# A planned attention and Fourier-gate kernel on one core: first head pair split, loads moved to the GpSimd queue, bit rows padded, new DMA model and new warm filling in the planner

## The chip, the cores and the metric

The kernel runs on 1 core of one Trainium2 chip. The metric is device time in microseconds, lower is better. A run is "fast" or "slow" by its state; only fast runs are compared. The profile is one execution: PE is TensorE, PEld its weight loads, DVE is VectorE, ACT is ScalarE, POOL is GpSimd, SP is SyncE. "SPq" or "POOLq" is an engine's sequencer, which issues DMAs.

## The reference, cut to what matters

```
# 4 batches x 8 heads, 768 positions, head size 64
q_bits = (q @ proj) > 0 ; k_bits = (k @ proj) > 0          # 6 bits each
mask   = bucket(q_bits) == bucket(k_bits)
attn   = softmax(where(mask, q @ k.T / 8, -1e9)) ; x = attn @ v
p      = x @ w_proj                                        # x1, x2, x3
y      = x1 * irfft(rfft(x2) * rfft(filter)) * x3
out    = y @ w_out
```

The kernel works on 16 pairs of heads. Four pairs make a batch; when a batch's four pairs are normalised, its projection, Fourier and output matmuls fill TensorE beside the attention of the next pairs.

## The kernel before

The kernel is recorded first and then ordered: a planner (`plan`) simulates the engines with a cost per instruction and a latency per DMA, decides the order on every engine, and the program is issued in that order. Each engine works through its instructions in the order in which they were issued (a profile below shows VectorE standing 7.24 us before its next one), so a latency that the planner believes too short puts an instruction where its engine must stand and wait. These are the parts that matter.

```
# the DMA model of the planner
LATE = (2600.0, 1900.0)
    if ty == "InstDmaTransposeAnt":
        return 1700.0, LATE[0], False, 0.0
    if ty == "InstDMACopy":
        move = n * partitions * bytes / 200.0          # one pipe of 200 GB/s
        own, late = {"Pool": (560.0, ...), "Activation": (150.0, ...)}.get(eng, (520.0, LATE[1]))
        return own, late, False, move
...
            x = end + 650
            if form["move"]:
                dma = max(x, dma) + form["move"]       # all queues share it
                got = dma + form["late"] - 650

# all loads on the SP queue ("p")
LOADS, SMALL, LOADQ = "p", "p", "p"

# high and low fp16 parts of q and k, then one DMA transpose each into the rows pr_q, pr_k
    def turn_dma(g):
        for which in ("k", "q"):
            nc.sync.dma_start_transpose(row[which]..., HLS[g][which]...)

# bits of the buckets, written under the 64 rows of q and k by 4 DMAs of 12 partitions
        for i in range(4):
            nc.load(row[...][HD : HD + NBIT, i % 2, :], bt[32 * i : 32 * i + NBIT, :], SMALL)

# normaliser: row sums S -> lt -> reciprocal rl -> DRAM rdr -> broadcast R, then the product on VectorE
    def finish(g):
        ...
            nc.load(lt[:, par, :], S[r0 : r0 + 1, 0:SEQ], SMALL)
        nc.vector.reciprocal(rl, rl)
        nc.load(rdr.rearrange("h (p c) -> p h c", p=P), rl, SMALL)
        for par in range(2):
            nc.load(R[HD * par : HD * par + HD, :], rdr[par : par + 1, :].to_broadcast([HD, SEQ]), SMALL)
        nc.vector.scalar_tensor_tensor(U, in0=T[:, 0:SEQ], scalar=vsd, op0=ALU.add, in1=R, op1=ALU.mult)
...                                                    # cut
```

The softmax here doesn't subtract the row's maximum and nothing guards it: scores larger than these inputs give would overflow.

## Time and profile before

| | before |
|---|---|
| time, median of the first 3 runs | 463.43 us (461.94 to 465.23) |
| span of the profiled run, mean granted clock | 461.0 us, 0.978 |
| PE busy | 431.6 us (94%) |
| useful matmul time (columns at full rate, worked out) | 381 us |

Lines of the page of the kernel before: busy time of two engines, and the DMA queues (packets, MB, share of the 16 DMA engines' span). q1 is the SP queue, q10 the ScalarE queue, q0 the GpSimd queue.

```profile
PE 431.6 (94%) x2590; PEld 233.4 (51%) x2590; DVE 305.9 (66%) x552; ACT 252.8 (55%) x348; POOL 112.2 (24%) x117
...
q1 hardware_dynamic: 99472, 51.00, 43.3%
q10 hardware_dynamic: 1552, 0.39, 0.4%
...
q0 software_dynamic: 128, 0.04, 0.0%
```

Nearly all bytes go through one queue, SP's, in small packets: 51.00 MB in 99472 packets is 513 B each.

Stretches of the kernel before: the length, busy time (instructions) of PE, PEld, DVE, ACT and POOL, the granted clock, the DMA share and GB/s.

```profile
20.00:30.00 10.00, 8.66 (x47) 3.81 (x46) 5.25 (x9) 6.71 (x9) 0.61 (x1) 0.63 0.86 181
80.00:90.00 10.00, 9.18 (x37) 3.75 (x37) 9.04 (x18) 3.65 (x6) 2.71 (x5) 0.83 0.64 159
260.00:280.00 20.00, 20.00 (x140) 12.10 (x139) 15.93 (x39) 11.94 (x18) 4.26 (x4) 1.00 0.21 60
```

The late part keeps PE busy without a gap at full clock; the early part does not, and its busy time holds warm-up matmuls and slow-clock matmuls.

The chain of work that ended last, from 10 to 140 us, its DMA transposes alone: start, length from issue to landing in us, and which.

```profile
12.38 3.31 DMA pr_k<-hl
18.05 4.62 DMA pr_q<-hl
28.36 3.21 DMA pr_q<-hl
54.82 4.45 DMA pr_q<-hl
71.54 4.34 DMA pr_q<-hl
118.44 3.37 DMA pr_k<-hl
```

A transpose on the chain takes 3.2 to 4.6 us, 3.88 us in the mean of the six. How long VectorE stood before its product with R, in total, times and the longest:

```profile
DVE R L232 <- DMA R<-rdr: 14.6, 6, 6.6
```

And the issues of the bit rows on SP, duration in ns as least, median and most:

```profile
L232 SPq DMA_DIRECT2D pr_q<-bt x30: 717/780/918, 24.9 to 333.2; - x30
L232 SPq DMA_DIRECT2D pr_k<-bt x30: 714/720/1072, 26.8 to 334.8; - x30
```

### The profile page before, as it was taken

To read this page: it belongs to the slowest core of one execution; us is meant where nothing else is said; L and a number is where in the kernel's file an instruction comes from. 1 tells how busy PE (TensorE), PEld (TensorE's weight loads), DVE (VectorE), ACT (ScalarE), POOL (GpSimd) and SP (SyncE) were. 2 spreads that over 40 slices of the span, in tenths; PEclk is the share of its full clock that TensorE was granted. 3 is DMA by queue.
4 is the path that set the end of the run, shared out by engine and by line. 5 is a ranking of instruction groups with operands and counts; after the bars stand their busy time and mean duration, and the time that the engine had idled before them with its cause. 6 is when DMAs were issued, how large, how long until landed. Compare 5 with 4: busy or idle time off the path is not lost.

```text
span 461.0 us, 7071 instructions
## 1 busy us (share of the span) xinstructions
PE 431.6 (94%) x2590; PEld 233.4 (51%) x2590; DVE 305.9 (66%) x552; ACT 252.8 (55%) x348; POOL 112.2 (24%) x117
## 2 busy tenths in 40 slices
PE   7688987969899999999999999999999999999996
PEld 5244544425355456544455665544556664445652
DVE  4667687949593899734588879225677873279870
ACT  5679979358146752777565766665666632200102
POOL 4103297223031521212232211113242010122000
PEclk9789999879999999999999999999999999999999
DMA  9988679798845324765372323451010103100003
GB/s 273 201 213 207 159 213 251 165 202 216 201 110 148 86 58 76 183 162 155 79 135 71 75 71 74 141 131 48 3 40 2 34 4 107 66 0 1 0 2 137
DMA packets 101187, 51.88 MB, mean 113 GB/s; under 512 B 83520, under 2 KB 92816, under 8 KB 101152
## 3 DMA queue, kind: packets, MB, share of 16 engines
q1 hardware_dynamic: 99472, 51.00, 43.3%
q10 hardware_dynamic: 1552, 0.39, 0.4%
q8 instruction: 20, 0.33, 0.3%
q14 instruction: 15, 0.12, 0.1%
q0 software_dynamic: 128, 0.04, 0.0%
HBM read 32.02 MB, written 6.39 MB: 83 GB/s over the span
## 4 chain that ended last, share of the span: by engine, by line
PE 71%; DMA 12%; DVE 9%; ACT 3%; issue 3%; SPq 1%; DVEq 0%; ACTq 0%; POOLq 0%
PE x L232 24%; PE pv L232 10%; PE stp L232 9%; PE wout L232 9%; PE x2b L232 6%; PE x2a L232 6%; DMA pr_q<-hl 4%; PE zps L232 2%; DMA lt<-S 2%; ACT pt L232 2%; DMA w<-in_moe_w_proj_dram 2%; PE fdft L232 2%; DMA pr_k<-hl 1%; DMA R<-rdr 1%; DMA rdr<-rl 1%
## 5 line engine op out<-in xcount | busy, mean ns | idle before, releaser
L232 ACT ACTIVATE pt<-stp,nmatch 128x768 f16<-128x768 f32 x192 | 168.6, 899 | 65.1 <-PE stp L232 62.4
L232 PE MATMUL stp<-pr_q,pr_k 76*128 76x512 f16 (+1 forms) x384 | 96.3, 334 | 11.2 <-ACT pt L232 8.5
L232 PE MATMUL x<-xh,wph 128*128 128x384 f16 x256 | 83.4, 326 | 0.5 <-DVE bt L232 0.2
L232 PE MATMUL x<-xl,wph 128*128 128x384 f16 x256 | 83.4, 326 | 0.0
L232 PE MATMUL x<-xh,wpl 128*128 128x384 f16 x256 | 83.4, 326 | 0.0
L232 PE MATMUL pv<-pt,vt 128*128 128x257 f16 (+1 forms) x384 | 76.4, 333 | 1.4 <-DVE bt L232 1.4
L232 PEld LDWEIGHTS <-wph 128*128 128x128 f16 x512 | 49.7, 97 | 34.6 <-issue 2.2
L232 DVE SCALAR_TENSOR_TENSOR T<-S,cst_sb,pv 64x512 f32<-64x512 f32 x64 | 38.3, 608 | 36.8 <-ACT S L232 35.9
L232 PEld LDWEIGHTS <-pr_k 76*128 76x128 f16 x384 | 36.9, 99 | 49.8 <-issue 22.8
L232 POOL TENSOR_TENSOR xl<-R,xh 128x768 f16<-128x768 f32 x16 | 26.3, 1641 | 133.1 <-DVE xh L232 112.4
L232 PEld LDWEIGHTS <-vt 128*128 128x128 f16 x384 | 37.8, 99 | 29.8 <-issue 5.9
L232 ACT COPY S<-pv 64x512 f32<-64x512 f32 (+1 forms) x48 | 22.8, 476 | 43.1 <-PE pv L232 39.1
L232 PEld LDWEIGHTS <-wpl 128*128 128x128 f16 x256 | 25.0, 97 | 16.1
L232 POOL TENSOR_TENSOR vt<-nat_v,vt 128x768 f16<-128x768 f32 x16 | 26.2, 1641 | 17.9 <-ACT vt L232 17.0
L232 PEld LDWEIGHTS <-xh 128*128 128x128 f16 x192 | 18.7, 97 | 20.7 <-issue 0.3
L232 DVE TENSOR_SCALAR bt<-zps,cst_sb 128x384 f16<-128x384 f32 x30 | 17.5, 610 | 16.2 <-PE zps L232 15.7
L232 ACT ACTIVATE osb<-wout 128x512 f32<-128x512 f32 x24 | 14.3, 596 | 24.7 <-PE wout L232 24.6
L232 POOL CAST vt<-nat_v 128x768 f16<-128x768 f32 x11 | 9.0, 823 | 74.1 <-PE pv L232 74.1
L232 DVE SCALAR_TENSOR_TENSOR R<-T,vsd,R 128x768 f32<-128x768 f32 x16 | 16.2, 1012 | 14.6 <-DMA R<-rdr 14.6
L232 DVE SCALAR_TENSOR_TENSOR hl<-nat_k,hl 128x768 f16<-128x768 f32 x16 | 16.3, 1016 | 12.2 <-ACT hl L232 12.1
L232 DVE TENSOR_TENSOR fu<-x2b,x2s 128x512 f32<-128x512 f32 x12 | 8.3, 688 | 23.6 <-PE x2b L232 23.6
L232 ACT ACTIVATE hl<-nat_k 128x768 f16<-128x768 f32 x16 | 13.5, 844 | 14.7 <-DMA pr_k<-hl 9.1
(339 smaller groups left out, 673.5 us busy)
## 6 DMA issues: line engine op xcount, KB each, us to landing
nat_k<-in_k_dram SPq DMA_DIRECT2D x16, 384.0 KB
nat_v<-in_v_dram SPq DMA_DIRECT2D x16, 384.0 KB
R<-rdr SPq DMA_DIRECT2D x32, 192.0 KB
out_dram<-osb SPq DMA_DIRECT2D x24, 256.0 KB
nat_q<-in_q_dram SPq DMA_DIRECT2D x15, 384.0 KB
w<-in_moe_w_proj_dram SPq DMA_DIRECT2D x12, 256.0 KB
w<-in_moe_filter_fft_dram SPq DMA_DIRECT2D x6, 256.0 KB
w<-in_moe_w_out_dram SPq DMA_DIRECT2D x4, 256.0 KB
```

The costliest lines, as they stand in the source:

```text
L232: o["done"] = getattr(getattr(nc, o["lane"]), o["method"])(*[sub(x) for x in o["args"]], **{n: sub(x) for n, x in o["kw"].items()})
```

## The change

Its intent: start the first pair head by head so that scores begin earlier; take the big loads off the SP queue, where they stand between transposes and normaliser; issue bit rows faster; give the planner a DMA model closer to the machine; and keep TensorE's clock up with filler matmuls in smaller pieces, without an end time.

```
+ROWS = 16
-LATE = (2600.0, 1900.0)
+DMA_LATE = (900.0, 1400.0)
+DMA_SHARE = 1.4
...
-        return 1700.0, LATE[0], False, 0.0
+        return 1500.0, DMA_LATE[0], False, 1900.0
-        move = n * partitions * bytes / 200.0
+        size = min(_run(wr[0]), _run(rd[0]))
+        move = n * partitions * bytes / size
+        move *= max(9.0, 11.0 + 0.0362 * size) / 16.0
...
+        return own, DMA_LATE[1] + (600.0 if eng == "Pool" else 0.0), False, max(60.0, move)
...
-                dma = max(x, dma) + form["move"]
-                got = dma + form["late"] - 650
+            x = max(s + 500.0 if form["late"] == DMA_LATE[0] else end + 300.0, dma.get(e, 0.0))
+            move = form["move"] * (DMA_SHARE if any(dma[y] > x for y in dma if y != e) else 1.0)
+            dma[e] = x + move                          # one pipe per queue
+            got = max(end, dma[e]) + form["late"]
...
-LOADS, SMALL, LOADQ = "p", "p", "p"
-WARM_COLS, WARM_UNTIL, WARM_FILL = 256, 115000.0, 0.7
+BITQ, WQ = "p", "g"
+LOADS, SMALL, LOADQ = "g", "p", "g"
+WARM_COLS, WARM_GAP, WARM_FILL = (256, 128, 64), 350.0, (0.97, 0.7)
...
-        load_qk(0, "p", "s")
+        for par in range(2):
+            first_loads(par)                           # k on SP, q and the identity on ScalarE, half a pair each
         NATS[0]["v"] = nat_load(v, 0, "v", "p")
-        hilo(0)
         load_qk(1, None, None)
-        turn_pe(0)
-        zbits(0, True)
+        for par in range(2):
+            first_turn(par)                            # high/low, transpose, bits, thresholds of one head
...
-                row[...][HD : HD + NBIT, i % 2, :], bt[32 * i : 32 * i + NBIT, :], SMALL
+                row[...][HD : HD + ROWS, i % 2, :], bt[32 * i : 32 * i + ROWS, :], BITQ
...                                                    # cut
```

More of the change, by code (lines that the diff above doesn't have):

```diff
@@ L168, in scale, with lower @@
         ])
+    def lower(self, out, a, c, b, lanes="v"):
+        self.either(*[
+            lambda e={"v": self.vector, "g": self.gpsimd}[x]: e.scalar_tensor_tensor(
+                out, in0=a, scalar=c, op0=ALU.mult, in1=b, op1=ALU.subtract
+            )
+            for x in lanes
+        ])
     def load(self, out, in_, lanes=None):
@@ L185, in inline_tensor, with fill @@
         return self.core.inline_tensor(data, name=name)
+    def fill(self, nc, bank, n, sub):
+        w, z = self.warm
+        nc.tensor.matmul(bank[:, SEQ : SEQ + n], sub(w), sub(z[:, 0:n]))
     def issue(self, tc, order, place):
@@ L228, in issue @@
                 if k < 0:
-                    nc.tensor.matmul(self.warm[0](real[bank]), sub(self.warm[1]), sub(self.warm[2]))
+                    self.fill(nc, real[bank], -k, sub)
                     continue
@@ L272, in _cols, with _run @@
     return n
+def _run(ap):
+    n = 1
+    for step, k in reversed(list(ap.ap)[1:]):
+        if step != n:
+            break
+        n *= k
+    return n * (2 if "16" in str(ap.dtype) else 4)
 def _cost(ins, eng, rd, wr):
@@ L287, in _cost @@
     if ty == "InstDmaTransposeAnt":
-        return 1700.0, LATE[0], False, 0.0
+        return 1500.0, DMA_LATE[0], False, 1900.0
     if ty == "InstDMACopy":
-        move = n * list(wr[0].ap)[0][1] * (2 if "16" in str(wr[0].dtype) else 4) / 200.0
-        own, late = {"Pool": (560.0, LATE[1] + 200.0), "Activation": (150.0, LATE[1] + 500.0)}.get(
-            eng, (520.0, LATE[1])
-        )
-        return own, late, False, move
+        size = min(_run(wr[0]), _run(rd[0]))
+        move = n * list(wr[0].ap)[0][1] * (2 if "16" in str(wr[0].dtype) else 4) / size
+        move *= max(9.0, 11.0 + 0.0362 * size) / 16.0
+        own = {"Pool": 560.0, "Activation": 480.0}.get(eng, 480.0)
+        if eng == "SP" and size == 2 * SEQ:
+            own = 600.0
+        return own, DMA_LATE[1] + (600.0 if eng == "Pool" else 0.0), False, max(60.0, move)
     big = [a for a in rd if _cols(a) > 1]
@@ L316, with HI_LANES, LO_LANES @@
 NQK = 4
-LOADS, SMALL, LOADQ = "p", "p", "p"
-WARM_COLS, WARM_UNTIL, WARM_FILL = 256, 115000.0, 0.7
+BITQ, WQ = "p", "g"
+LOADS, SMALL, LOADQ = "g", "p", "g"
+WARM_COLS, WARM_GAP, WARM_FILL = (256, 128, 64), 350.0, (0.97, 0.7)
 T_SET = (1.5, 3.0, 5.0)
+def HI_LANES(g, which):
+    return "v" if g == 0 and which == "q" else "s"
+HL1_AT = -1.52
+def LO_LANES(g, which):
+    return "v"
 def PROJ_AT(b, x):
@@ L390, in plan @@
             last[x] = g[0]
+            for m in g[1:]:
+                deps[m].add(g[0])
         if ops[g[0]]["method"] == "matmul" and len(g) > 2 and not ops[g[0] + 1]["with_"]:
@@ L422, in _order @@
     port = {"DVE": 0.0, "Pool": 0.0}
-    dma = 0.0
+    dma = {}
     forced = {}
@@ L525, in _order @@
             gap = s - free[e]
-            if book.warm is not None and s < WARM_UNTIL and gap > 350.0 and before:
+            if book.warm is not None and gap > 40.0 and before:
                 w0 = free[e]
-                room = w0 + WARM_FILL * gap
-                while True:
-                    c = WARM_COLS / 2.4
-                    if active.get(int(w0 // 3413) - 1, 0.0) < 1640.0:
-                        c *= 2
-                    if w0 + c > room:
-                        break
-                    active[int(w0 // 3413)] = active.get(int(w0 // 3413), 0.0) + WARM_COLS / 2.4
-                    extra.append((w0, -1, before))
-                    w0 += c
+                while w0 < s:
+                    cold = active.get(int(w0 // 3413) - 1, 0.0) < 1640.0
+                    if not cold and gap < WARM_GAP:
+                        break
+                    room = free[e] + WARM_FILL[0 if cold else 1] * gap - w0
+                    c = [n for n in WARM_COLS if n / (1.2 if cold else 2.4) <= room]
+                    if not c:
+                        break
+                    x = int(w0 // 3413)
+                    active[x] = active.get(x, 0.0) + c[0] / 2.4
+                    extra.append((w0, -c[0], before))
+                    w0 += c[0] / (1.2 if cold else 2.4)
             mode[0] = o["mode"]
@@ L552, in _order @@
         if form["late"]:
-            x = end + 650
-            if form["move"]:
-                dma = max(x, dma) + form["move"]
-                got = dma + form["late"] - 650
-            else:
-                got = end + form["late"]
+            x = max(s + 500.0 if form["late"] == DMA_LATE[0] else end + 300.0, dma.get(e, 0.0))
+            move = form["move"] * (DMA_SHARE if any(dma[y] > x for y in dma if y != e) else 1.0)
+            dma[e] = x + move
+            got = max(end, dma[e]) + form["late"]
         for t in o["touch"]:
@@ L646 @@
     ident = cp.tile([P, P], FP16, name="ident")
-    nc.gpsimd.dma_start(ident, id_d.ap())
     for r0 in (0, HD):
@@ L658 @@
     wps = psS.tile([P, 1024], FP32, tag="s", name="stp")
-    nc.warm = (lambda t: t[:, SEQ : SEQ + WARM_COLS], warm[:, 0:P], warm[:, 0:WARM_COLS])
+    nc.warm = (warm[:, 0:P], warm)
     nc.at = -2.9
-    nc.tensor.matmul(nc.warm[0](wps), nc.warm[1], nc.warm[2])
+    nc.tensor.matmul(wps[:, SEQ:1024], *nc.warm)
     NPR = 3
@@ L709, in hilo @@
         HLS[g] = {}
-        nc.at = g - 1.6
+        nc.at = g - 1.6 if g > 1 else HL1_AT
         for which in ("k", "q"):
@@ L713, in hilo @@
             hl = hlp.tile([P, 2 * NCH, 2, HD], FP16, tag=f"hl_{which}", name="hl")
-            if g == 0 and which == "q":
-                nc.vector.tensor_scalar(hl[:, :, 0], nat, QKS, None, ALU.mult)
-            else:
-                nc.scalar.mul(hl[:, :, 0], nat, QKS)
-            nc.vector.scalar_tensor_tensor(
-                hl[:, :, 1], in0=nat, scalar=QKS, op0=ALU.mult, in1=hl[:, :, 0], op1=ALU.subtract
-            )
+            nc.scale(hl[:, :, 0], nat, QKS, HI_LANES(g, which))
+            nc.lower(hl[:, :, 1], nat, QKS, hl[:, :, 0], LO_LANES(g, which))
             HLS[g][which] = hl
@@ L730, in turn_dma @@
             )
-    def turn_pe(g):
-        row = prs[g % NPR]
-        for which in ("k", "q"):
-            for par in range(2):
-                tp = psW.tile([P, SEQ], FP16, tag="w", name="tp")
-                for n in range(NCH):
-                    nc.tensor.transpose(
-                        tp[:, ts(n, P)],
-                        HLS[g][which][:, NCH * par + n].rearrange("p s d -> p (s d)"), ident,
-                    )
-                if par:
-                    nc.vector.tensor_copy(row[which][:, par], tp)
-                else:
-                    nc.scalar.copy(row[which][:, par], tp)
@@ L747, in zbits, with first_loads @@
-    def zbits(g, direct=False):
+    def first_loads(par):
+        hs = slice(NCH * par, NCH * par + NCH)
+        for which, src in (("k", k), ("q", q)):
+            if par == 0:
+                NATS[0][which] = natp.tile(
+                    [P, 2 * NCH, HD], FP32, tag="qk", name=f"nat_{which}", bufs=NQK
+                )
+            t_ = NATS[0][which]
+            if which == "k":
+                nc.load(
+                    t_[:, hs].rearrange("p n d -> p (n d)"),
+                    src[0, par].rearrange("(p n) d -> p (n d)", n=NCH), "p",
+                )
+            else:
+                nc.load(t_[:, hs], src[0, par].rearrange("(n p) d -> p n d", p=P), "s")
+            if par == 0 and which == "q":
+                nc.load(ident, id_d.ap(), "s")
@@ new lines, in first_turn @@
+    def first_turn(par):
+        row = prs[0]
+        hs = slice(NCH * par, NCH * par + NCH)
+        for which in ("k", "q"):
+            nc.at = -2.0 + 0.5 * par
+            nat = NATS[0][which]
+            if par == 0:
+                HLS[0][which] = hlp.tile([P, 2 * NCH, 2, HD], FP16, tag=f"hl_{which}", name="hl")
+            hl = HLS[0][which]
+            nc.scale(hl[:, hs, 0], nat[:, hs], QKS, "sv")
+            nc.vector.scalar_tensor_tensor(
+                hl[:, hs, 1], in0=nat[:, hs], scalar=QKS, op0=ALU.mult, in1=hl[:, hs, 0],
+                op1=ALU.subtract,
+            )
+            tp = psW.tile([P, SEQ], FP16, tag="w", name="tp")
+            for n in range(NCH):
+                nc.tensor.transpose(
+                    tp[:, ts(n, P)], hl[:, NCH * par + n].rearrange("p s d -> p (s d)"), ident
+                )
+            for hf in range(2):
+                cs = slice(HALF * hf, HALF * hf + HALF)
+                nc.copy(row[which][:, par, cs], tp[:, cs], "sv")
+        zps = psW.tile([P, HALF], FP32, tag="w", name="zps")
+        srcs = [(w_, hf) for w_ in ("k", "q") for hf in range(2)]
+        for s_ in range(2):
+            for i, (which, hf) in enumerate(srcs):
+                nc.tensor.matmul(
+                    zps[32 * i : 32 * i + 32, :], pjh[:, s_],
+                    row[which][:, par, HALF * hf : HALF * hf + HALF],
+                    start=(s_ == 0), stop=(s_ == 1),
+                )
+                nc.ops[-1]["with_"] = bool(s_ or i)
+        for i in (0, 2, 3, 1):
+            which, hf = srcs[i]
+            r_ = slice(32 * i, 32 * i + ROWS)
+            nc.vector.tensor_scalar(
+                row[which][HD : HD + ROWS, par, HALF * hf : HALF * hf + HALF],
+                zps[r_, :], thresh[r_, :], BIT, ALU.is_gt, ALU.mult,
+            )
@@ L748, in zbits @@
+    def zbits(g):
         row = prs[g % NPR]
@@ L763, in zbits @@
                     nc.ops[-1]["with_"] = bool(hf or s_ or i)
-        if not direct:
-            for hf in range(2):
-                nc.vector.tensor_scalar(
-                    bt[:, HALF * hf : HALF * hf + HALF], zs[hf], thresh, BIT, ALU.is_gt, ALU.mult
-                )
-        if direct:
-            for i in (2, 0, 3, 1):
-                for hf in range(2):
-                    r_ = slice(32 * i, 32 * i + NBIT)
-                    nc.vector.tensor_scalar(
-                        row[("q", "k")[i // 2]][HD : HD + NBIT, i % 2, HALF * hf : HALF * hf + HALF],
-                        zs[hf][r_, :], thresh[r_, :], BIT, ALU.is_gt, ALU.mult,
-                    )
-            return
+        for hf in range(2):
+            nc.vector.tensor_scalar(
+                bt[:, HALF * hf : HALF * hf + HALF], zs[hf], thresh, BIT, ALU.is_gt, ALU.mult
+            )
         for i in range(4):
             nc.load(
-                row[("q", "k")[i // 2]][HD : HD + NBIT, i % 2, :], bt[32 * i : 32 * i + NBIT, :], SMALL
+                row[("q", "k")[i // 2]][HD : HD + ROWS, i % 2, :], bt[32 * i : 32 * i + ROWS, :], BITQ
             )
@@ L791 @@
     prog = [0.0]
-    KR = slice(0, HD + NBIT)
+    KR = slice(0, HD + ROWS)
     xh = {}
@@ L877, in attn_gen @@
     def attn_gen():
-        load_qk(0, "p", "s")
+        nc.at = -2.5
+        NATS[0] = {}
+        HLS[0] = {}
+        for par in range(2):
+            first_loads(par)
         NATS[0]["v"] = nat_load(v, 0, "v", "p")
-        hilo(0)
         load_qk(1, None, None)
-        turn_pe(0)
-        zbits(0, True)
+        for par in range(2):
+            first_turn(par)
         hilo(1)
@@ L1015, in load_p @@
             piece[key] = stg.tile([P, DM], FP32, tag="xs", name="w32", bufs=NXS)
-            nc.load(piece[key], src)
+            nc.load(piece[key], src, WQ)
         def wsrc(c, third):
```

## The prediction

> **What bounds the kernel now.** TensorE, but only from about 180 us on. The table of windows shows it busy 20.0 of every 20 us from 180 to 280 us; before that 6 to 9.7 us in each 10, part of it warm-up matmuls, and the granted clock drops to 0.63 (20-30 us) and 0.78-0.88 (80-110 us). Counting matmul columns at full rate, useful work is an estimated 381 of the 461 us. First score matmul of each head pair, from the trace: pair 0 at 14.7 us, pair 1 at 30.4, pair 5 at 91.3, pair 6 at 129.7, pair 9 at 206.3. Span minus useful work is about 45 us before pair 5, 14 from pair 5 to 6, 6 from 6 to 9, and 11 in the remaining 255 us. So the gain has to come from the first 130 us.
>
> There the chain of waits runs through the SP queue: 18% of it is DMA transposes, 11% small normaliser DMAs, 6% a weight load, 4% the identity load. SP issues nearly everything in order (about 0.5 us each, bit rows 0.8, transposes 1.4-2.4), and a load that waits for its buffer holds up the transposes behind it. DMA engines are 85-110% busy in most 10 us windows to 100 us (256 B packets take 18 ns, 1536 B 65 ns). ScalarE sets a floor of twelve exponentials of 0.90 us and two high-part scalings of 0.84 us: 12.5 us per early pair.
>
> **What the change does.**
> 1. Startup by head: half-size loads, identity off the 5.5 us GpSimd path, half copies, three thresholds of 0.57 us ahead of the first scores. First score at about 10 us; pair 1 at 23-24.
> 2. Loads on the GpSimd queue: SP keeps transposes, bit rows, normaliser and output; the loads' waiting moves to GpSimd, which is only 24% busy. Trainium skill, "DMA: Bandwidth & Descriptors", section "Issuing engines are not separate DMA queues": all queues use the same 16 DMA engines, so I count issue time and blocking, not bandwidth. The early DMA work (76 us of packet time by pair 5) then becomes the next limit: pair 5 at about 80 us.
> 3. Bit rows at 16 partitions: issue near 0.5 us instead of 0.8, about 1.2 us of SP per pair.
> 4. New DMA model and warm filling reorder instructions; useful matmul work is identical, and from pair 9 the TensorE order is the same. I expect a higher clock to 110 us.
>
> **Sum.** Pair 5 about 11 us earlier, pairs 5 to 6 in 32 us instead of 38: pair 6 at about 112 us (-17); 3 to 6 us more from clock and order, late stages unchanged. Predicted 441 us, 8 in 10 between 430 and 453. Faster by over 2%: 0.89; within 2%: 0.08; slower: 0.03.
>
> **What would show it.** Right: first score near 10 us; less waiting on SP ahead of transposes; pair 6 near 112 us; pair 9 to the end still 250-256 us. Wrong on 2 if GpSimd shows several us per q load (1536 pieces of 256 B), or loads wait there behind tensor work.
>
> **What would make it wrong.** Descriptor writing on GpSimd may grow with pieces (the small loads took 0.5-0.7 us), or starve while VectorE holds the shared port (Trainium skill, "SBUF — State Buffer", section "SBUF: two separate sides", the "DVE blocks DMA" trap; no run here shows it yet). Then early pairs stay near 15 us and the result is 450-465 us. If two queues overlap better than I count, 430.

## The result, and the profile after

The changed kernel is slower: 494.94 us in the median (490.97 to 496.12, 4 runs) against 462.94 us (461.94 to 465.23, 4 runs). The ratio is 1.0669, with a 95% interval of 1.0593 to 1.0744. Here and below a ratio is the mean time of one kernel's fast runs over that of the other's fast runs of the same rounds, so it is not quite the ratio of the quoted medians. All ratios are to the kernel before, run on the same chip in the same rounds.

The profile after, same lines of the page:

```profile
PE 441.6 (89%) x2622; PEld 238.4 (48%) x2622; DVE 317.3 (64%) x555; ACT 253.3 (51%) x351; POOL 167.4 (34%) x191
...
q1 hardware_dynamic: 64496, 26.85, 23.6%
q0 software_dynamic: 7248, 24.52, 17.9%
q10 hardware_dynamic: 1712, 0.43, 0.4%
```

The bytes now go through two queues of very unlike packets. q0 carries 24.52 MB in 7248 packets, 3.4 KB each in the mean; the packet records of the trace show loads as packets of 4096 B (median 185 ns) and 4608 B, where the transposes beside them on q1 are packets of 256 B (18 ns).

```profile
20.00:30.00 10.00, 4.67 (x19) 2.09 (x17) 1.99 (x3) 4.58 (x6) 3.02 (x5) 1.00 1.24 184
80.00:90.00 10.00, 9.58 (x67) 5.29 (x66) 7.83 (x11) 8.40 (x11) 9.93 (x11) 0.90 0.46 108
260.00:280.00 20.00, 18.38 (x108) 10.10 (x107) 14.62 (x25) 10.44 (x15) 9.53 (x9) 1.00 0.28 85
```

PE is down to 4.67 us of 10 between 20 and 30 us, although the clock is now full, and there are holes in the late part too, where the DMA engines are only 0.28 busy. The transposes of the chain from 10 to 130 us, and the broadcasts R that have come into it:

```profile
17.14 8.47 DMA pr_k<-hl
27.57 7.96 DMA pr_k<-hl
37.83 5.93 DMA pr_k<-hl
70.41 4.91 DMA R<-rdr
86.49 6.14 DMA R<-rdr
101.36 4.86 DMA R<-rdr
126.36 6.08 DMA R<-rdr
```

A transpose now takes 5.9 to 8.5 us. VectorE stands before R at every one of the 16 pairs:

```profile
DVE R L245 <- DMA R<-rdr: 57.8, 16, 7.5
```

What the two engines do around one such wait in the late part; first VectorE (start, length, instruction, and in brackets the idle time before it and what ended it), then SP:

```profile
320.58 0.42 DVE L245 TENSOR_SCALAR rl<-lt 128x12 f32<-128x12 f32 x1 [0.39 <-issue]
321.04 0.23 DVE L245 RECIPROCAL rl<-rl 128x12 f32<-128x12 f32 x1
328.51 1.02 DVE L245 SCALAR_TENSOR_TENSOR R<-T,vsd,R 128x768 f32<-128x768 f32 x1 [7.24 <-DMA R<-rdr]
...
321.30 0.39 SPq L245 DMA_DIRECT2D rdr<-rl  x1
322.70 0.36 SPq L245 DMA_DIRECT2D out_dram<-osb  x1
323.79 1.12 SPq L245 DMA_DIRECT2D R<-rdr  x2
```

The product with R is the very next VectorE instruction after the reciprocal. No other VectorE work is ordered between them while the value goes to DRAM and comes back, so VectorE stands for 7.24 us, and all that is ordered behind it stands too.

Such a wait is not yet lost time. In the kernel before, VectorE stood about as long after the same reciprocal, but for another value, and R had landed when its product came 0.66 us later:

```profile
298.72 0.74 DVE L232 SCALAR_TENSOR_TENSOR T<-S,cst_sb,pv 64x512 f32<-64x512 f32 x1 [7.44 <-ACT S L232]
```

Over the whole run the waits for R grew by 43.2 us while the waits of T for S fell from 35.9 to 11.6 us. In the stretch shown TensorE had other matmuls and was busy throughout. What the waits cost shows where TensorE in turn stands for VectorE. Its waits after 200 us in the changed kernel, in total, times and the longest:

```profile
PE idrq L245 <- DVE T L245: 3.7, 2, 2.3
PE fdft L245 <- DVE T L245: 3.0, 2, 1.6
PE x L245 <- DVE T L245: 1.0, 1, 1.0
```

These sum to 7.7 us, all after pair 9's start, and the kernel before has none of them there.

The step that did work shows in the bit rows:

```profile
L245 SPq DMA_DIRECT2D pr_q<-bt x30: 531/557/1426, 32.8 to 363.7; - x30
L245 SPq DMA_DIRECT2D pr_k<-bt x30: 527/557/591, 34.2 to 364.9; - x30
```

Start of the first score matmul of a pair, read from the traces, in us (the last column is the span from pair 9 to the end):

| kernel | pair 0 | pair 1 | pair 5 | pair 6 | pair 9 | pair 9 to end |
|---|---|---|---|---|---|---|
| before | 14.7 | 30.4 | 91.3 | 129.7 | 206.3 | 254.7 |
| after | 15.5 | 38.1 | 102.3 | 139.7 | 230.0 | 264.3 |

Of the 33.3 us of span, 23.7 are lost by pair 9 and 9.6 after it. So there are at least two questions: what slows the loaded early part, and what slows the late part, where DMA is nearly idle.

### The profile page after: what moved, and what is told of

Its sections match the earlier page's. It is cut to its first block, busy times and chain, and to the rows that moved or that the text cites. A ratio compares the mean times of both kernels' runs of the same rounds, so it can differ in the third digit from the quotient of the medians.

```text
span 494.3 us, 7153 instructions
## 1 busy us (share of the span) xinstructions
PE 441.6 (89%) x2622; PEld 238.4 (48%) x2622; DVE 317.3 (64%) x555; ACT 253.3 (51%) x351; POOL 167.4 (34%) x191
## 3 DMA queue, kind: packets, MB, share of 16 engines
q0 software_dynamic: 7248, 24.52, 17.9%
## 4 chain that ended last, share of the span: by engine, by line
PE 43%; DMA 26%; DVE 20%; ACT 4%; issue 4%; SPq 2%; POOL 1%; DVEq 0%; ACTq 0%; POOLq 0%
PE x L245 14%; DMA R<-rdr 10%; PE wout L245 7%; PE pv L245 5%; DMA rdr<-rl 5%; PE stp L245 5%; DMA pr_k<-hl 5%; DMA lt<-S 4%; PE x2a L245 4%; PE x2b L245 3%; DVE T L245 2%; DVE R L245 2%; SPq L245 2%; DVE rl L245 2%; ACT pt L245 2%
## 5 line engine op out<-in xcount | busy, mean ns | idle before, releaser
L245 PE MATMUL stp<-pr_q,pr_k 80*128 80x512 f16 (+1 forms) x384 | 99.2, 343 | 9.8 <-ACT pt L245 8.9
L245 PE MATMUL x<-xh,wph 128*128 128x384 f16 x256 | 85.1, 332 | 13.5 <-DVE T L245 12.4
L245 PE MATMUL x<-xl,wph 128*128 128x384 f16 x256 | 85.2, 333 | 0.0
L245 PE MATMUL x<-xh,wpl 128*128 128x384 f16 x256 | 85.0, 332 | 0.0
L245 POOL TENSOR_TENSOR xl<-R,xh 128x768 f16<-128x768 f32 x16 | 28.7, 1791 | 113.0 <-DVE xh L245 104.5
L245 PEld LDWEIGHTS <-pr_k 80*128 80x128 f16 x384 | 37.5, 101 | 47.9 <-issue 21.6
L245 PEld LDWEIGHTS <-vt 128*128 128x128 f16 x384 | 38.1, 100 | 33.7 <-issue 9.7
L245 DVE SCALAR_TENSOR_TENSOR T<-S,cst_sb,pv 64x512 f32<-64x512 f32 x64 | 37.9, 608 | 12.6 <-ACT S L245 11.6
L245 ACT COPY S<-pv 64x512 f32<-64x512 f32 (+1 forms) x47 | 22.5, 478 | 33.7 <-PE pv L245 29.6
L198 PE MATMUL stp<-warm 128*128 128x256 f16 (+2 forms) x157 | 24.7, 292 | 1.2 <-ACT pt L245 1.2
L245 DVE SCALAR_TENSOR_TENSOR hl<-nat_k,hl 128x768 f16<-128x768 f32 (+1 forms) x17 | 16.6, 976 | 12.6 <-ACT hl L245 12.5
L245 POOL DMA_DIRECT2D nat_k<-in_k_dram x15 | 10.8, 718 | 39.2 <-DVE hl L245 32.7
L245 POOL DMA_DIRECT2D nat_q<-in_q_dram x15 | 15.6, 1041 | 22.7 <-DVE hl L245 11.9
```

The source lines that it names most:

```text
L198: nc.tensor.matmul(bank[:, SEQ : SEQ + n], sub(w), sub(z[:, 0:n]))
L245: o["done"] = getattr(getattr(nc, o["lane"]), o["method"])(*[sub(x) for x in o["args"]], **{n: sub(x) for n, x in o["kw"].items()})
```

## The experiments

Three theories. Q: loads in a second queue are served in turn with the small urgent transfers of SP and make them late. M: the new DMA model believes R too early, so the planner puts its product too early on VectorE. S: the split start (or the filling) loses time itself. Every part of the change can be put in or out of the kernel, and with all parts out the program is instruction for instruction the kernel before on all five engines. The part called the split also holds an earlier place in the plan for pair 1's high and low parts. Where "same order" is said, only the issuing engine of the loads was changed after planning, and the compute order was compared and found identical.

### Same order as after, loads issued from SP

```
+                lane = o["lane"]
+                if lane == "gpsimd" and (a load of q, k, v, weights or tables, not of the first pair):
+                    lane = "sync"
-                o["done"] = getattr(getattr(nc, o["lane"]), o["method"])(
+                o["done"] = getattr(getattr(nc, lane), o["method"])(
```

> The changed kernel, every engine's compute instructions in exactly its order; only the q, k, v, weight and table loads after the first pair are issued from SP instead of GpSimd. Theory Q (two queues share the DMA engines, the GpSimd queue's 4 KB packets stand between the 256 B and smaller packets of transposes and normaliser): the transposes before 130 us land in about 4 us instead of 5.5 and the time falls to 470-482 us. Theory M (the new DMA model orders VectorE so that it reaches the normaliser product too early): the wait of R on VectorE stays over 40 us and the time stays at 488-500 us. Theory S (the first-pair split is the loss): pair 1 still starts near 38 us.

Measured: 487.94 us, ratio 1.0551 (1.0502 to 1.0599). The urgent DMAs recover as Q says: from issue to landing between 10 and 130 us, in medians, pr_k transposes 5.93 to 3.57 us, R 4.75 to 3.50, lt 4.88 to 2.58 (pr_q, less, 5.13 to 4.13). Pair 1 starts at 35.5 us, between the 38 of theory S and the 30.4 of before. But the time comes down only to the edge of what M says, because VectorE's wait for R stays at 53.4 us, and pair 9 to the end stays at 264.2 us. Lateness of the queue is not the cause of the late loss.

### Same order as before, loads issued from GpSimd

The same edit on the kernel before, from "sync" to "gpsimd".

> The kernel before, compute order unchanged; the same loads are issued from GpSimd instead of SP. Theory Q: transposes before 130 us take 5 us and more, pair 9 starts over 10 us later than 206, time 475-490 us. Theory M: 458-466 us, because the order is the old one. If freeing the SP queue is worth what I predicted, it is faster: 445-455 us.

Measured: 483.36 us, 1.0416 (1.0352 to 1.0480). Pair 9 starts at 225.1 us, 18.8 later than before, and pair 9 to the end is 256.8 us. The freed SP queue gave no gain. Chain of this kernel, 10 to 140 us, its transposes and then two of its GpSimd pieces:

```profile
13.06 8.77 DMA pr_k<-hl
32.59 6.58 DMA pr_q<-hl
60.87 9.46 DMA pr_q<-hl
104.29 8.96 DMA pr_q<-hl
133.33 7.74 DMA pr_q<-hl
...
88.90 0.56 POOL w L235
89.48 1.66 POOL xl L235
```

8.30 us in the mean against 3.88, with the same compute order. That overstates the typical transpose, because each chain holds only those that were waited for: over all 16 transposes issued from 10 to 140 us the mean went from 4.22 to 5.87 us and the longest from 8.10 to 9.71. (The views give no landing times for kernels with 12 bit rows, because a transfer of 12 partitions leaves 13 semaphore updates in the trace where the others leave 16; counted so, the landings agree with every transpose of the two chains.) Wait for R: 15.0 us, as before.

The move of the loads is thus worth 4.2% without theory M. It is not lateness of transposes alone. The last lines show that load issues now also stand in GpSimd's stream ahead of its compute (xl): from 10 to 206 us GpSimd's pieces take 8.8 us of the chain, where the chain of the kernel before has none. And until pair 9 starts TensorE is idle for 37.5 us instead of 24.1 and busy for 187.6 instead of 182.2, at a mean granted clock of 0.901 instead of 0.950. How the 18.8 us divide among these is not shown.

### After, with the old DMA model

The model's lines of the diff taken back; the planner orders anew.

> The changed kernel with the old DMA model in the planner, all else as changed (loads on GpSimd, first pair split, 16 bit rows, new warm filling); the order is planned anew. Theory M: VectorE waits for R fall from 58 us to under 25 and the time to 465-475 us; from pair 9 to the end again about 255 us. Theory Q: the early loss stays, 480-490 us.

Measured: 496.50 us, 1.0733 (1.0679 to 1.0787), above both expectations. Its two halves are each as a theory says: the wait for R is 15.6 us and pair 9 to the end 256.6 us, so the late loss is the model's. But pair 9 starts at 238.7 us, worse than after. With the loads on GpSimd, transposes up to 130 us landed in medians of 5.16 us (k) and 6.98 us (q) and at most in 16.8 and 18.9 us. The new model is bad for R, but the old one, combined with the second queue, is no better for the early part.

### Before, with the new DMA model alone

> The kernel before with only the new DMA model in the planner. Theory M: VectorE waits for R rise from 15 us to 35 or more and the time is 475-490 us, pair 9 to end about 264 us. Theory Q alone: 460-467 us.

Measured: 478.29 us, 1.0356 (1.0280 to 1.0432). Wait for R:

```profile
DVE R L232 <- DMA R<-rdr: 43.2, 14, 8.8
```

This is M alone, within what it expected, but the loss is less in the late part (258.5 us, not 264) and more by pair 9 (215.7 us, 9.4 later).

### The queues by themselves

A test program without the kernel's work: per stretch one transpose, one row read lt and two broadcasts R from SP, beside three loads of 384 KB.

```
for ph, eng in enumerate((None, None, "gpsimd", "gpsimd", "scalar", "scalar", "sync", "sync")):
    ...                                   # VectorE copies: all of the last stretch has landed
    if eng is not None:
        e.dma_start(K, ...); e.dma_start(Q, ...); e.dma_start(V, ...)
    nc.sync.dma_start_transpose(rows[ph]..., hl...)
    nc.sync.dma_start(L, S[32:33, 0:SEQ])
    for par in range(2):
        nc.sync.dma_start(R[64 * par : 64 * par + 64, :], rdr[par : par + 1, :].to_broadcast([64, SEQ]))
```

> A test program, wrong result on purpose: eight stretches, each with one transpose of 128 x 1536 fp16 (393 KB), one normaliser row read (24 B pieces) and two broadcasts R, all issued from SP; beside them three loads (k, q, v, 384 KB each) from nobody (2 stretches), from GpSimd (2), from ScalarE (2), and from SP ahead of the transpose (2). Theory Q (packets of the GpSimd queue are 4 KB and are served in turn with the small ones of SP): transpose alone lands in 3.3 to 3.8 us, beside GpSimd loads in 6 to 9 us, beside ScalarE loads, whose packets are 256 and 1536 B, in 4.5 to 6 us, and R likewise 3.2 alone and over 4.5 beside GpSimd. If the loss were only GpSimd's blocked instruction stream, the transpose would land in under 4.5 us in every stretch but the SP one.

Measured (the result is wrong on purpose; one look). From issue to landing, two stretches each, in us:

| three loads from | transpose | lt | R (second of the two) |
|---|---|---|---|
| nobody | 3.78, 3.68 | 2.44, 2.50 | 3.56, 3.39 |
| GpSimd | 9.06, 4.79 | 10.11, 6.91 | 9.79, 6.33 |
| ScalarE | 6.70, 6.07 | 6.38, 5.66 | 5.43, 4.67 |
| SP, ahead of them | 5.51, 5.84 | 2.51, 3.19 | 3.56, 3.57 |

The view of the row tile gives the same for the transposes, least, median and most: alone, then beside GpSimd loads.

```profile
DMA to landing us min/median/max: 3.7/3.7/3.8
...
DMA to landing us min/median/max: 4.8/6.9/9.1
```

No compute stands in GpSimd's stream here, so a blocked instruction stream isn't needed to make these transfers late (in the kernel it comes on top, as the chain above shows). An estimate: three loads are 1.15 MB, 17 packets of 4.2 KB for each of 16 engines, at about 0.18 us 3.1 us of work that a transpose may have to share; its median grew by 3.2 us. The 9.06 of the first GpSimd stretch is more than that and came with a k load that itself took 8.9 us; why, is left open. Loads ahead in the same queue also delay the transpose, but the reads behind it keep their 2.5 to 3.6 us. But they were also issued later, about 5 us after the first load, since the transpose ahead of them took 2.9 to 3.1 us to issue instead of 1.3 to 1.6. Counted from the first load's issue the last R is there after 10.0 and 9.6 us with SP, 9.4 and 9.0 with ScalarE, 13.0 and 9.5 with GpSimd. So the test shows that transfers in flight together make each other late; that one queue protects the small ones in the kernel, because their place among the loads is then fixed, is argued and not shown.

### Before, same order, loads issued from ScalarE

The same edit again, to "scalar": a second queue, but hardware packets of at most 2048 B.

> The kernel before in its compute order, the same loads issued from ScalarE: a second queue like that of GpSimd, but with packets of 256 to 2048 B, not 4 KB. If a second queue as such slows the transposes: they take over 5.5 us in the chain and the time is 475-490 us, as with GpSimd. If it needs the 4 KB packets: transposes 4 to 5 us. ScalarE's own issue time and waits for free buffers may cost here by themselves, so the transposes' times count, not the total.

Measured: 474.71 us, 1.0273 (1.0214 to 1.0331), with transposes on the chain of 6.04, 6.29, 4.62 and 5.16 us, 5.53 in the mean: just over the line drawn, with the time just under the range that went with it. A second queue as such costs (3.88 to 5.53); GpSimd's costs more (8.30). Over all 16 transposes from 10 to 140 us the means are 4.22, 4.63 and 5.87 us, the same order with smaller steps. The size of its packets is one visible difference, but the profile also lists GpSimd's queue as another kind (software_dynamic, not hardware_dynamic), and other compute stands behind the loads; the runs do not separate these.

### After with the loads back on SP, planned anew

```
-BITQ, WQ = "p", "g"
-LOADS, SMALL, LOADQ = "g", "p", "g"
+BITQ, WQ = "p", "p"
+LOADS, SMALL, LOADQ = "p", "p", "p"
```

> The changed kernel with all loads back on the SP queue, planned anew with the new DMA model. Theory Q: the early part gains, 475-485 us, but the last part (pair 9 to the end) stays near 264 us because of the model. Theory that the loss needs the two together: 463-470 us.

Measured: 478.87 us, 1.0325 (1.0263 to 1.0387), in the range of Q. The last part is 261.8 us and the wait for R 52.9 us, both the model's.

### Only R later in the new model

```
+        slow = 2000.0 if (the two broadcasts R from rdr) else 0.0
-        return own, DMA_LATE[1] + (600.0 if eng == "Pool" else 0.0), False, max(60.0, move)
+        return own, DMA_LATE[1] + slow + (600.0 if eng == "Pool" else 0.0), False, max(60.0, move)
```

On the kernel before with the new model:

> The kernel before with the new DMA model, but the model's latency of the two broadcasts R made 2 us longer, nothing else. Theory M (R is what the new model places too early): VectorE waits for R fall under 20 us, pair 9 to the end back to 254-257 us, time 462-470 us. If other latencies of the model matter more: stays 474-482 us.

Measured: 465.18 us, 1.0079 (1.0005 to 1.0152); pair 9 to the end 256.2 us.

```profile
DVE R L232 <- DMA R<-rdr: 9.3, 4, 6.6
```

One latency for one kind of DMA takes the model's loss from 3.6% to 0.8%. By the model's constants both halves of R are there about 3.2 us after the first is issued (0.48 issue, 0.30, 0.49 for each half, 1.4), where the old model says 4.4. In the late part of the changed kernel VectorE could start 3.9 to 4.9 us after that issue, early 5.5 to 7.4.

With all latencies 1.5 us longer instead (`DMA_LATE = (2400.0, 2900.0)`):

> The kernel before with the new DMA model and every DMA 1.5 us later in it. Theory M: 458-468 us, with R waits under 20 us. If not the latencies but the shape of the model (one pipe per queue, packet sizes) is at fault: 472-482 us.

Measured: 466.45 us, 1.0094 (1.0031 to 1.0156), wait for R 21.3 us, a little over the line. The same repair by a coarser means.

The coarse repair on the changed kernel, loads still on GpSimd:

> The changed kernel with every DMA 1.5 us later in its model; loads stay on GpSimd. Theory Q and M as two separate causes: the late part is mended (pair 9 to the end 254-257 us), the early loss stays, 478-488 us. If too short latencies were all of it: 465-472 us.

Measured: 473.45 us, 1.0230 (1.0157 to 1.0303), between the two ranges; one of the four runs was slow (478.82 us) and is left out of the ratio. Pair 9 to the end is 257.6 us and the wait for R 17.7 us; transposes up to 130 us still take 6.8 (k) and 6.6 us (q). Honest latencies regain 4.4 of 6.7 points, more than the model's own part; that the planner then also leaves room for the late transposes is the likely reason, not a tested one.

The fine repair on the changed kernel:

> The changed kernel with only R 2 us later in its model; loads stay on GpSimd. Theory that the two causes add: pair 9 to the end 254-258 us, R waits under 25 us, transposes before 130 us still over 5 us, 474-484 us.

Inconclusive. Three of its four runs, the profiled one too, were slow (490.36 to 492.70 us); the one fast run took 480.76 us, in the expected range.

### What is left when both causes are undone

After, with loads on SP and R mended:

> The changed kernel with both suspected causes undone and nothing else: loads back on SP, and only R 2 us later in the new DMA model. If the two causes are complete: 458-468 us, ratio to before 0.99 to 1.01. If something else of the change loses time (split, filling, rows): over 470 us.

Measured: 468.56 us, 1.0145 (1.0087 to 1.0203). This lies between the two ranges. So the two causes are not all: 1.5% remain. The mended model alone had left 0.8%, so the remainder may lie in the rest of the model as well as in the split, the filling or the rows.

The split alone on the kernel before:

> The kernel before with the first-pair split alone. First scores at 10-12 us instead of 14.7; 457-464 us. If the split is a cause of the loss: over 468 us with pair 1 later than 30.4 us.

Measured: 463.90 us, 1.0018 (0.9974 to 1.0062): no gain, no loss. The first scores come at 13.9 us, not 10 to 12, and pair 1 at 35.5, later than 30.4; what the first head gains the next pair gives back: its transposes are issued at 16.51 and 18.79 us instead of 12.38 and 18.05, because its high and low parts now stand behind the second head's work (ScalarE's first of them starts at 13.36 us, not 9.99). Pair 6 starts at 107.1 us, 22.6 earlier than before, and yet pair 9 at 205.9 as before.

The split with the mended model, as a candidate:

> Kernel before with the first-pair split and the new DMA model mended at R; loads on SP, 12 bit rows, old filling. Candidate for a faster version: 455-464 us; over 466 us if the gain of the split is not kept.

Measured: 469.10 us, 1.0153 (1.0093 to 1.0214). The candidate failed.

The padded rows alone (`ROWS = 16`, planned anew):

> Kernel before with only the bit rows padded to 16. I had predicted about 1.2 us of SP time per pair: issue of one row block 0.55 us instead of 0.75; time 458-464 us, so no clear gain since SP is not always what is waited for.

Measured: 456.40 us, 0.9896 (0.9825 to 0.9967): faster than both kernels and below the expected range, a gain clear of noise but under 2%. The planner had also changed the order, since 16 partitions cost more than 12 in its model. To keep the order, the rows were priced as 12:

```
+        rows = list(wr[0].ap)[0][1]
-        move = n * list(wr[0].ap)[0][1] * (2 if ...
+        move = n * (12 if rows == 16 else rows) * (2 if ...
```

> Kernel before with the bit rows padded to 16 and every engine's order exactly as before. If the padding itself is what gained 1% (shorter issue on SP): ratio 0.985 to 0.995. If it was the new order that the planner made of it: 0.997 to 1.003.

Measured with 5 rounds: 456.60 us, 0.9876 (0.9842 to 0.9909), every engine's order as before.

```profile
L245 SPq DMA_DIRECT2D pr_q<-bt x30: 517/554/1283, 25.1 to 326.9; - x30
L245 SPq DMA_DIRECT2D pr_k<-bt x30: 538/539/1448, 26.4 to 328.2; - x30
```

The padding itself gains. 30 issues are shorter by 780 - 554 ns and 30 by 720 - 539 ns, 12.2 us of SP time, against 5.8 us by which the median time is lower. Pair 9 starts at 200.0 us instead of 206.3, so the gain lies in the early part.

The rows and the new filling:

> Kernel before with 16 bit rows and the new warm filling. If the filling loses what is left over when the two causes are undone: 463-470 us against 456.4 with the rows alone. If it is harmless: 454-460 us, and the split is what is left.

Measured: 462.21 us, 1.0022 (0.9982 to 1.0061), between the two ranges. Against the rows alone that is 1.0022 / 0.9896 = 1.013, and against the rows in the same rounds (kept order) 1.0022 / 0.9876 = 1.015. The filling does what it is for, the granted clock of the profiled run is 0.995 against 0.980, and still loses. That its matmuls stand in TensorE's in-order stream ahead of real work is one possible way: until pair 9 filler keeps TensorE busy for 33.7 us instead of 20.3. But the planner also ordered anew, and the order of the other instructions differs on every compute engine from that of the rows alone. No run has the filling at the old order, so which of the two loses is open.

First-pair split, rows and filling together, loads on SP and old model:

> The kernel before with the first-pair split, 16 bit rows and the new warm filling; loads on SP and the old DMA model. Theory Q and M together explain the loss: this is free of it and slightly faster than before, 455-463 us. If the split or the filling lose time of their own: 468-480 us.

Measured: 468.09 us, 1.0103 (1.0054 to 1.0153), at the lower edge of the range in which the split or the filling lose. With this run the whole way from before to after is measured, a part at a time:

| kernel | ratio to before | step |
|---|---|---|
| before | 1 | |
| rows of 16 | 0.9896 | -1.0% |
| + filling | 1.0022 | +1.3% |
| + split start | 1.0103 | +0.8% |
| + new DMA model | 1.0325 | +2.2% |
| + loads on GpSimd (= after) | 1.0669 | +3.3% |

The runs are of different rounds and chips and each ratio is uncertain by about half a point, so the two small middle steps are rough. The parts also depend on each other: alone, the model costs 3.6% and the queue 4.2%, while at the order of after the loads' return to SP regains only 1.2 of the 6.7 points (1.0669 to 1.0551).

## Why the prediction was wrong, point by point

- Where the gain had to come from was right: the early part, where the rows gain theirs. The sign of the whole was wrong. The sum also took an early pair 6 to be kept to the end ("pair 6 at about 112 us (-17)", "late stages unchanged"). Three kernels reach that mark, the split alone (107.1 us), the rows with the filling (112.3) and these with the split (112.3), and none is faster than before; with the split alone the whole lead is gone by pair 9.
- Step 1, the split. Predicted first scores at about 10 us and pair 1 at 23 to 24; measured 15.5 and 38.1. Two terms failed. The scaling of `pj`, for which VectorE stood 2.56 us until a GpSimd load landed 5.05 us after its issue, was ordered ahead of q's low part. And pair 1's transposes, issued at 17.14 and 18.82 us, took 8.47 and 11.75 us beside GpSimd's loads. Even without those loads (the split alone) it gains nothing.
- Step 2, the loads on GpSimd, is the step that failed most. "So I count issue time and blocking, not bandwidth" took the Trainium skill, "DMA: Bandwidth & Descriptors", section "Issuing engines are not separate DMA queues", to mean that another queue could only help. The same page says in "Queues, rings and completion order" that each DMA engine goes round its queues a packet at a time. The runs agree in effect, though none shows the turns themselves: with the same compute order the transposes of the chain went from 3.88 to 8.30 us, all of them from 4.22 to 5.87. In one queue the loads' waiting for free buffers may have been a pacing, which I read as blocking alone; no run tests that. With only the loads moved, pair 5 came 16.6 us later (107.9) and pair 9 18.8 us later, where I had pair 5 11 us earlier; in the changed kernel pair 5 came 11.0 us later.
- Step 3, the rows: the mechanism was right (an issue of 0.72 to 0.78 us came down to 0.56). The size was 0.8 us of SP per pair (12.2 us over 15 pairs), not 1.2, and yet it was worth 1.2% alone at the same order, more than I expected when I ran it. It is the only part that pays.
- Step 4, the model and filling: I counted a gain of 3 to 6 us "from clock and order" without pricing the model. I had seen that the TensorE order from pair 9 on was the same and concluded "late stages unchanged"; VectorE's order had changed, R's product stood next to its reciprocal, and the late part lost 9.6 us. The higher clock to 110 us did come in the profiled run (0.91 to 0.95) and brought no gain; from 110 to 206 us the clock was lower (1.00 to 0.93), so over the whole span it did not rise (0.978 to 0.972).
- What I named as the danger, slow descriptor writing, is not it: a q load of 1536 pieces takes GpSimd 1.04 us of issue and a k load 0.72. No run here shows the starvation by VectorE that the Trainium skill, "SBUF — State Buffer", warns of.

```profile
L245 POOL DMA_DIRECT2D nat_k<-in_k_dram x15 | 10.8, 718 | 39.2 <-DVE hl L245 32.7
L245 POOL DMA_DIRECT2D nat_q<-in_q_dram x15 | 15.6, 1041 | 22.7 <-DVE hl L245 11.9
```

The groups of the page of after: after the count, busy us, mean ns of one, and the idle time before. GpSimd's loads do wait, 32.7 us for VectorE to free the k buffers, but that wait is not what slowed the transposes of the test program. What it cost the kernel is not shown.

## What to carry to other kernels

Before moving bulk loads to another queue, look at what small, urgent transfers share the DMA engines with them: one in-order queue may be what keeps those transfers quick, and the engine that takes the loads has its own work behind them. When a planner's latencies change, compare the order on every in-order engine and not only on the busiest one; here a value believed about 1 us too early went with a wait of 3.6 us in the mean at each of 16 pairs. Then ask which of these waits the busiest engine had to share: in the late part that was 7.7 us. Take a bundle of changes apart: here one part of five gained 1.2%, one did nothing measurable alone, and the other three hid the gain.

## What the Trainium skill lacked or had wrong

- "DMA: Bandwidth & Descriptors", "Issuing engines are not separate DMA queues": it says that several issuing engines only save issue time. It lacks the price: with unchanged compute order, loads in a second queue stretched the transposes of the chain from 3.88 us to 5.53 (ScalarE) and 8.30 us (GpSimd), all transposes from 10 to 140 us from 4.22 to 4.63 and 5.87 us, and the kernel by 2.7% and 4.2%.
- The same page, "SWDGE vs HWDGE vs iDMA", calls packets of the software path preferably at most 4096 B. The trace holds 2400 packets of 4608 B (three pieces of 1536 B) beside 3104 of 4096 B. It does not say what such packets do to a neighbour queue of 256 B packets.
- The same page, "Why a DMA increments its semaphore by 16 and not by 1", lets one work out that 12 partitions use 12 engines and 16 use 16, and that the sequencer writes the rest of the semaphore. The trace of before agrees: its 60 bit row transfers leave 180 semaphore updates fewer than 16 each, that is 13 each, and with 16 rows none is missing. It has no time for it on this chip: the issue took 0.72 to 0.78 us with 12 partitions and 0.54 to 0.55 us with 16, and the padding gained 1.2%.
- No page has the issue time of GpSimd loads by pieces: 0.55 us for 128 pieces of 2048 B, 0.72 us for 256 of 1536 B, 1.04 us for 1536 of 256 B.
- "TensorE: Matmul & The Clock Gate" explains how activity opens the clock. The runs add that filling can lose: with the new filling the granted clock was 0.995 instead of 0.980 and the time 1.3% longer, with an order planned anew.
